# Attention values in two arrangements: partition halves exchanged by SP's DMA queue in place of VectorE copies

## The chip, the cores and the metric

The kernel runs on one core of a Trainium2 chip. A core has TensorE (PE: matrix multiplications from SBUF into PSUM), VectorE (DVE) and ScalarE (ACT) for elementwise work and for moving PSUM to SBUF, GpSimd (POOL) and SyncE (SP), here used to issue DMAs. Each engine runs its own instructions in order; semaphores order work between engines. DMAs issued by SP are carried out in the background by 16 DMA engines, which all queues share. SBUF and PSUM have 128 partitions; elementwise engines here read and write the same partition numbers or whole halves of 64. The metric is the device time of one execution, in microseconds (us).

## The reference

Inputs are q, k, v of shape (8 batches, 12 heads, 448 rows, 64) and three weights. For each batch and head

```python
scores = scale * np.matmul(q, k.transpose(0, 1, 3, 2))   # scale = 1/sqrt(64)
attn = np.maximum(scores, 0.0) ** 2 / S                  # S = 448
return np.matmul(attn, v)
```

The heads' outputs stand side by side as x of shape (8*448, 768), and the second part is

```python
gate = np.maximum(x @ w_gate, 0.0)      # 768 -> 1536
val = x @ w_val
return (gate * val @ w_out)             # 1536 -> 768, float32
```

## The kernel before

**Tiling.** Matmuls are done four at a time on the 64x64 quarters of the PE array (`mm4`, all through line 72). Two heads make a pair, two pairs a quad; a batch has three quads (qd 0 to 2). A score tile (`tile_of`, 21 in a batch, seven for each quad) is one `mm4` of 64x448 blocks into a pair of PSUM banks. `relu2` evacuates it: ACT takes the relu into an `r_sb` buffer (line 232), DVE squares it into `attn` (line 233). `r_sb` has four buffers (pool `rpool`), and a new relu needs a buffer whose last user has finished.

**Values.** When a quad's seven score tiles are done, seven `mm4` (28 matmuls, `value_passes`) accumulate its 128x2x448 values in a pair of PSUM banks. For batches 1 to 5, `values` evacuates them to `x0`, the first bank by ACT (line 266), the second by DVE (line 267); the gate and value matmuls also need `x1`, the same data with the two partition halves exchanged. `exchange` makes it with two DVE copies of 64x896 bf16 (line 261). Batch 0 is done by `first_batch`, which evacuates by itself and then calls `exchange`. For the last two batches, 6 and 7, `values_by_parity` makes two other arrangements: `even`, which holds the low half's values in both halves, and `odd`, which holds the high half's in both. Each engine evacuates its bank in two instructions, low half to `even` and high half to `odd` (lines 276 and 277), then DVE copies each across (lines 278 and 279).

**The order of the work.** The order on every engine is the program's (`pin`). Each body of the loop over batches (line 746) runs the gate and value units of the batch before (`gv_unit`: 12 steps of one `mm4`, then a relu on ACT at line 320 and a product on DVE at line 321) and, between their steps, the score tiles and values of the batch itself. `paced` places these events evenly. A value event of a quad stands two score tiles behind the quad's last one. Score tiles and value banks take turns in PSUM at banks 0-1 and 2-3 (`sc_later`), so each waits for the evacuation of the one two before it. In body 5 the attention of batch 6 begins early: (6,0), which is batch 6, quad 0, goes into a place in `kn_b[1]`; batch 7's x arrangements use `kr` and `qr`.

**Transposes.** From batch 2 on, q and k are regrouped on DVE (line 180, into `kr` and `qr`) and transposed into `T_b` by DMA transposes that SP issues: eight a batch, at places given by `turned` for batches 2, 4, 5, 6 and 7, and at the end of body 2 for batch 3. POOL issues most loads; a small POOL copy (`hold`, line 677) waits for a batch's transposes, and the next loads stand behind it. SP also stores half of the result in `out_pair` (line 409).

**The rest.** `out_pair` is the last product, done for two batches at once; batches 6 and 7 use a scheme with fewer products, prepared by `token_sums` and computed by `gv_pair`, which read the `even` and `odd` arrangements.

Of the kernel before, what the change touches and what calls it, by code (L numbers as in the profile page):

```python
# [10 lines left out]
BF16 = mybir.dt.bfloat16  # L11
AF = mybir.ActivationFunctionType
ALU = mybir.AluOpType
# [3 lines left out]
def kernel(  # L17
# [22 lines left out]
    nc = tc.nc  # L40

    B, H, S, D = q.shape
# [5 lines left out]
    NQ = HP // 2  # L48
# [4 lines left out]
    lam = 1.0 / (D * S)  # L53
# [5 lines left out]
    rpool = ctx.enter_context(tc.tile_pool(name="rpool", bufs=4))  # L59
# [6 lines left out]
    HALVES = [(c, slice(c * 64, c * 64 + 64)) for c in range(2)]  # L66

    def pin(ins):
        return tc.keep_in_program_order(ins)
# [181 lines left out]
    def value_passes(b, qd, ps, i0, i1):  # L251

        attn, v_sb = attn_of(b, qd), v_b[b % NB]
        for i in range(i0, i1):
            mm4([ps[:, r, :S] for r in range(2)], lambda r, c: v_sb[:, 2 * qd + c, i, :],
                lambda r, c: attn[:, 2 * i + c, :], i == 0, i == NC - 1)

    def exchange(b, qd):
        x0, x1 = (x_of[b][e][qd] for e in range(2))
        for (_, p), (_, other) in zip(HALVES, HALVES[::-1]):  # L260
            pin(nc.vector.tensor_copy(x1[p], x0[other]))  # L261

    def values(b, qd, ps):
        value_passes(b, qd, ps, 0, NC)
        x0 = x_of[b][0][qd]
        pin(nc.scalar.activation(x0[:, 0, :], ps[:, 0, :S], AF.Copy))  # L266
        pin(nc.vector.tensor_copy(x0[:, 1, :], ps[:, 1, :S]))
        exchange(b, qd)

    def values_by_parity(b, qd, ps):  # L270

        value_passes(b, qd, ps, 0, NC)
        even, odd = (x_of[b][e][qd] for e in range(2))
        lo, hi = (p for _, p in HALVES)
        for x, p in ((even, lo), (odd, hi)):
            pin(nc.scalar.activation(x[p, 0, :], ps[p, 0, :S], AF.Copy, scale=float(lam)))
            pin(nc.vector.tensor_scalar(x[p, 1, :], ps[p, 1, :S], float(lam), None, ALU.mult))
        pin(nc.vector.tensor_copy(even[hi], even[lo]))
        pin(nc.vector.tensor_copy(odd[lo], odd[hi]))
# [315 lines left out]
    def first_batch(units):  # L595
# [53 lines left out]
        passes(1, 4)  # L649
        value_passes(0, 2, both, 4, NC)  # L650
        exchange(0, 0)
        exchange(0, 1)
        pin(nc.scalar.activation(x_of[0][0][2], both[:, :, :S], AF.Copy))
        exchange(0, 2)
# [181 lines left out]
```

## Time and profile before

| what | value |
|---|---|
| median of 3 runs | 406.9 us (406.57 to 408.36) |
| profiled execution, its own time | 406.69 us |
| its span, first to last instruction | 404.9 us |
| PE busy | 393.0 us, 97% |
| DVE busy | 303.9 us, 75% |
| ACT busy | 244.3 us, 60% |
| SP's DMA queue (q1) | 13.99 MB, 17.9% of 16 engines |

The page gives, for each engine, the busy time and its share of the span; then groups of instructions by line, with what they wrote and read (`x<-x` is a tile x written from a tile x), how many there were, the time that they kept the engine busy, the mean length of one in ns, and the idle time before them with what ended it. A timeline lists instructions in order of start: start, length, engine, line, operation, output and inputs, shapes, and how many were merged; in square brackets stand the idle time before and the instruction or DMA that ended it. "SPq" is an instruction in SP's sequence, so its length is the time to issue a DMA; the landing is listed apart.

### The profile page before, as it was taken

Reading aid. Unit: us, or ns where it says so; the run is one execution under the profiler, and the core shown is the slowest. Engines: PE = TensorE matmul, PEld = TensorE weight load, DVE = VectorE, ACT = ScalarE, POOL = GpSimd, SP = SyncE. Lnnn points to the kernel's source line nnn. Section 1 sums busy time; section 2 is a strip of 40 time slices with the busy share of each in tenths; the row PEclk is TensorE's granted clock in tenths of the full one; section 3 lists DMA queues with packets and bytes.
Section 4 is the critical chain, followed back from the end, with each engine's and each line's share of the span. In section 5 each row is a group of like instructions: output and inputs, shape, how many; then the busy total and the mean of one; then the engine's idle time right before and its main releaser. Section 6 shows DMA issues by size and latency. Waiting matters only on the chain.

```text
span 404.9 us, 16604 instructions
## 1 busy us (share of the span) xinstructions
PE 393.0 (97%) x7392; PEld 276.3 (68%) x7392; DVE 303.9 (75%) x532; ACT 244.3 (60%) x358; POOL 96.0 (24%) x164
## 2 busy tenths in 40 slices
PE   7899999999999999999999999999999999999994
PEld 3567767779776666666677677687777766777773
DVE  5985895599944786787833988988889869997651
ACT  3962984797334776877324889899873243434221
POOL 8833500610213601205244030020003120000240
PEclk9999999999999999999999999999999999999999
DMA  9999999799726993978946459561002350000154
GB/s 157 176 196 196 197 194 135 122 203 162 119 83 177 118 161 70 139 112 99 191 86 173 103 88 123 103 95 14 3 3 50 83 145 3 3 2 3 42 135 101
DMA packets 90984, 44.17 MB, mean 109 GB/s; under 512 B 55424, under 2 KB 89952, under 8 KB 90912
## 3 DMA queue, kind: packets, MB, share of 16 engines
q0 software_dynamic: 51136, 28.58, 49.5%
q1 hardware_dynamic: 39104, 13.99, 17.9%
q8 instruction: 58, 0.95, 0.9%
q10 hardware_dynamic: 672, 0.54, 0.5%
q14 instruction: 14, 0.11, 0.1%
HBM read 47.19 MB, written 11.01 MB: 144 GB/s over the span
## 4 chain that ended last, share of the span: by engine, by line
PE 79%; DVE 7%; DMA 5%; ACT 3%; issue 2%; SPq 2%; POOL 0%; DVEq 0%; ACTq 0%; POOLq 0%
PE ps L72 78%; DVE attn L233 4%; DMA kn<-in_k_dram 3%; ACT r_sb L232 3%; SPq L409 2%; DMA qn<-in_q_dram 1%; PE ps L208 1%; DMA out_dram<-attn 1%; DVE x L640 1%; DVE attn L399 0%; DVE kqT L209 0%; DVE hT L321 0%; ACT g_sb L320 0%; DVE kr L180 0%; DVE qr L180 0%
## 5 line engine op out<-in xcount | busy, mean ns | idle before, releaser
L72 PE MATMUL ps<-x,gv 64*64 64x448 bf16 x3552 | 203.5, 349 | 0.5 <-ACT r_sb L232 0.3
L72 PEld LDWEIGHTS <-gv 64*64 64x64 bf16 x4032 | 139.0, 107 | 54.8 <-issue 2.8
L232 ACT ACTIVATE r_sb<-ps 128x896 bf16<-128x896 f32 x167 | 147.9, 926 | 18.6 <-PE ps L72 15.1
L233 DVE TENSOR_TENSOR attn<-r_sb 128x896 bf16<-128x896 bf16 x167 | 102.2, 623 | 31.3 <-ACT r_sb L232 24.5
L72 PE MATMUL ps<-kqT 64*64 64x448 bf16 x672 | 67.9, 351 | 3.8 <-ACT r_sb L232 2.8
L72 PEld LDWEIGHTS <-hT 128*64 128x64 bf16 x1056 | 56.2, 110 | 20.8 <-issue 1.7
L409 POOL DMA_DIRECT2D out_dram<-attn x60 | 31.6, 531 | 154.0 <-DVE attn L399 121.2
L395 ACT ACTIVATE attn<-ps 128x384 f32<-128x384 f32 x64 | 28.9, 451 | 63.9 <-PE ps L72 63.3
L72 PE MATMUL ps<-wo,hT 128*64 128x384 bf16 (+1 forms) x720 | 53.9, 306 | 0.0
L321 DVE TENSOR_TENSOR hT<-ps,g_sb 128x448 bf16<-128x448 f32 x72 | 44.5, 619 | 9.2 <-ACT g_sb L320 8.6
L320 ACT ACTIVATE g_sb<-ps 128x448 bf16<-128x448 f32 x72 | 39.2, 546 | 18.5 <-PE ps L72 18.1
L399 DVE TENSOR_TENSOR attn<-ps,attn 128x384 f32<-128x384 f32 (+1 forms) x48 | 22.7, 503 | 33.4 <-ACT attn L395 19.4
L72 PEld LDWEIGHTS <-vn 64*64 64x64 bf16 (+1 forms) x840 | 30.9, 107 | 12.8 <-issue 2.3
L72 PEld LDWEIGHTS <-kqT 64*64 64x64 bf16 x672 | 27.0, 106 | 18.4 <-issue 8.4
L72 PE MATMUL ps<-attn,vn 64*64 64x448 bf16 x672 | 36.9, 350 | 0.1
L513 ACT ACTIVATE kqT<-ps 128x896 f32<-128x896 f32 x18 | 16.5, 918 | 25.0 <-PE ps L72 25.0
L116 POOL DMA_DIRECT2D vn<-in_v_dram x36 | 23.8, 681 | 23.0 <-DMA wo<-in_moe_w_out_dram 9.6
L677 POOL COPY flag<-kqT 128x1 bf16<-128x1 bf16 x12 | 3.1, 261 | 103.0 <-DMA kqT<-kr 75.9
L72 PE MATMUL ps<-o_ring,hT 128*64 128x384 bf16 (+1 forms) x336 | 25.8, 306 | 0.1
L517 DVE TENSOR_TENSOR kqT<-ps,kqT 128x896 f32<-128x896 f32 x18 | 19.5, 1084 | 5.9 <-PE ps L72 4.2
L266 ACT ACTIVATE x<-ps 128x448 bf16<-128x448 f32 x15 | 8.2, 544 | 14.4 <-PE ps L72 14.4
L261 DVE COPY x<-x 64x896 bf16<-64x896 bf16 x36 | 14.7, 408 | 2.0
(104 smaller groups left out, 289.4 us busy)
## 6 DMA issues: line engine op xcount, KB each, us to landing
out_dram<-attn SPq DMA_DIRECT2D x48, 96.0 KB, 2.6
out_dram<-attn POOLq DMA_DIRECT2D x46, 96.0 KB, 2.4
kn<-in_k_dram POOLq DMA_DIRECT2D x7, 384.0 KB, 5.9
qn<-in_q_dram POOLq DMA_DIRECT2D x7, 384.0 KB, 7.8
vn<-in_v_dram POOLq DMA_DIRECT2D x14, 192.0 KB, 9.1
gv<-in_moe_w_gate_dram POOLq DMA_DIRECT2D x6, 384.0 KB, 11.3
gv<-in_moe_w_val_dram POOLq DMA_DIRECT2D x6, 384.0 KB, 10.9
wo<-in_moe_w_out_dram POOLq DMA_DIRECT2D x2, 1152.0 KB, 12.3
```

What stands on the lines that cost most here:

```text
L72: pin(nc.tensor.matmul(o, lhsT=l, rhs=r, start=start, stop=stop, skip_group_check=True))
L116: pin(nc.gpsimd.dma_start(out=o, in_=i))
L232: pin(nc.scalar.activation(r, src, AF.Relu))
L233: pin(nc.vector.tensor_tensor(dst, r, r, ALU.mult))
L261: pin(nc.vector.tensor_copy(x1[p], x0[other]))
L320: pin(nc.scalar.activation(g_sb, o[0], AF.Relu, scale=float(out_scale)))
L321: pin(nc.vector.tensor_tensor(hT[:, mf, col:col + S], o[1], g_sb, ALU.mult))
L395: pin(nc.scalar.activation(out_of(t, r, c), bank(P, t), AF.Copy))
L399: pin(nc.vector.tensor_tensor(o, bank(Q, t), o, ALU.add))
L409: pin(engines[c].dma_start(out=rows[:, c0:c1, :], in_=src))
L513: pin(nc.scalar.activation(held(n, j), both(PQ[n][0]), AF.Copy))
L517: pin(nc.vector.tensor_tensor(k, both(PQ[n][1]), k, ALU.add))
```

## The change

`exchange` issues its two copies as DMAs from SP for quads 0 and 1 of batches 1 to 5. Batch 0 and quad 2 of every batch keep DVE's copies.

`values_by_parity` evacuates both banks once over all 128 partitions, ACT the first and DVE the second, into a tile `both` that is allocated from `rpool` under the name `r_sb`; four DMAs from SP then copy each half of `both` to both halves of `even` or `odd`. Quad 2 of batch 7, the last, keeps the way of before.

```diff
     def exchange(b, qd):
         x0, x1 = (x_of[b][e][qd] for e in range(2))
         for (_, p), (_, other) in zip(HALVES, HALVES[::-1]):
-            pin(nc.vector.tensor_copy(x1[p], x0[other]))
+            if b > 0 and qd < NQ - 1:
+                pin(nc.sync.dma_start(out=x1[p], in_=x0[other]))
+            else:
+                pin(nc.vector.tensor_copy(x1[p], x0[other]))
...
         value_passes(b, qd, ps, 0, NC)
         even, odd = (x_of[b][e][qd] for e in range(2))
+        if (b, qd) != (B - 1, NQ - 1):
+            both = rpool.tile([128, 2, S], BF16, name="r_sb")
+            pin(nc.scalar.activation(both[:, 0, :], ps[:, 0, :S], AF.Copy, scale=float(lam)))
+            pin(nc.vector.tensor_scalar(both[:, 1, :], ps[:, 1, :S], float(lam), None, ALU.mult))
+            for x, (_, p) in zip((even, odd), HALVES):
+                for _, o in HALVES:
+                    pin(nc.sync.dma_start(out=x[o], in_=both[p]))
+            return
         lo, hi = (p for _, p in HALVES)
```

## The prediction

> **What bounds the kernel now.** I read the page first, then the chain of waits, then the timelines of SP, ACT and PE around the places that the change touches.
>
> ```profile
> span 404.9 us, 16604 instructions
> PE 393.0 (97%) x7392; PEld 276.3 (68%) x7392; DVE 303.9 (75%) x532; ACT 244.3 (60%) x358; POOL 96.0 (24%) x164
> ...
> L261 DVE COPY x<-x 64x896 bf16<-64x896 bf16 x36 | 14.7, 408 | 2.0
> ...
> out_dram<-attn SPq DMA_DIRECT2D x48, 96.0 KB, 2.6
> ```
>
> TensorE is busy for 97% of the span and DVE for 75%. So DVE time that is taken away is worth only what TensorE waits for DVE; every new wait of TensorE is paid in full. A DVE exchange copy takes 0.41 us, a plain copy issued by SP lands 2.6 us after its issue.
>
> The timeline of SP (start, length, what) has two places where the new copies get in behind transposes:
>
> ```profile
> 55.81 8.52 SPq L188 DMA_TRANSPOSE kqT<-kr  x4
> 64.38 7.10 SPq L188 DMA_TRANSPOSE kqT<-qr  x4
> ...
> 254.04 5.95 SPq L188 DMA_TRANSPOSE kqT<-kr  x4
> 260.08 6.03 SPq L188 DMA_TRANSPOSE kqT<-qr  x4
> ```
>
> SP issues in order, and eight transposes hold it for 12.1 us (254.04 to 266.11). The timelines of ACT and of PE in that stretch:
>
> ```profile
> 257.53 1.10 ACT L276 ACTIVATE kn<-ps 64x448 bf16<-64x448 f32 x2 [0.35 <-PE ps L72]
> 258.65 0.92 ACT L232 ACTIVATE r_sb<-ps 128x896 bf16<-128x896 f32 x1
> 260.23 0.92 ACT L232 ACTIVATE r_sb<-ps 128x896 bf16<-128x896 f32 x1 [0.66 <-PE ps L72]
> 261.05 0.54 ACT L320 ACTIVATE g_sb<-ps 128x448 bf16<-128x448 f32 x1
> 261.56 2.67 ACT L232 ACTIVATE r_sb<-ps 128x896 bf16<-128x896 f32 x3
> 264.12 0.55 ACT L320 ACTIVATE g_sb<-ps 128x448 bf16<-128x448 f32 x1
> 264.54 1.75 ACT L232 ACTIVATE r_sb<-ps 128x896 bf16<-128x896 f32 x2
> ```
>
> ```profile
> 259.82 0.38 PE L72 MATMUL ps<-kqT 64*64 64x448 bf16 x2 [0.63 <-DVE kn L277]
> ...
> 264.79 0.51 PE L72 MATMUL ps<-kqT 64*64 64x448 bf16 x4
> ...
> 265.53 1.52 PE L72 MATMUL ps<-attn,vn 64*64 64x448 bf16 x28
> ```
>
> The value bank of batch 6, quad 0 (written (6,0) below) is evacuated at 257.5, in the middle of the transposes of batch 7. Five relus of score tiles follow it: 258.65, 260.23, and three from 261.56; then, after a g_sb, those of tiles 14 and 15.
>
> **The change, part by part.** The compiled order of PE and of POOL is unchanged; DVE loses 24 rows, ACT four; SP gains 40 copies of 64x896 bf16 (112 KB each, 4.6 MB).
>
> *Work removed.* 20 exchange copies x 0.408 = 8.2 us of DVE. In five value banks two copies (0.39 each) and one of two TENSOR_SCALARs (0.62): 5 x 1.4 = 7.0 us of DVE; one of two 0.54 us activations: 2.7 us of ACT. DVE should fall from 303.9 to about 289, ACT to 241.6. On the path of this I find the 0.63 us above (TensorE waits for the second TENSOR_SCALAR; used below), 0.46 us at 287.77 (a score tile waits for a relu behind the two activations), some 0.3 us at 277 (the same kind) and some 0.4 us in gaps of 0.1 to 0.2 at 61, 238, 294 and 302. Together -1.2 us besides the 0.63; bounds 0 and -2.
>
> *(A) The bank copy of (6,0).* The new tile `both` is one of the four r_sb buffers, and its four DMAs must land before the buffer is used again. In the compiled order it is the fifth relu after it (tile 13) that waits for these four DMAs; in the trace that relu starts at 263.3. The DMAs stand in SP's order behind batch 7's transposes. Last transpose done with issuing: 266.12. SP's stores to HBM are the nearest row for a plain copy: 0.55 us each, 0.62 from start to start, so the fourth starts at 268.03. They landed after 1.9 to 4.2 us, median 2.2 in the stretch from 212 to 224; with 2.3 the buffer is free at 270.3, and tile 13's relu ends 0.92 later, at 271.25. Tile 15 writes the same PSUM banks as tile 13. It would have come at 264.79 - 0.65 = 264.14 (without the wait for the second TENSOR_SCALAR), and now waits until 271.25. Behind it on ACT are the g_sb and tile 14's relu, done at 272.6; the values of (6,1) need that one's banks. They began at 265.53 before: 7.1 us later.
>
> TensorE then stood still for about 7 us, and its clock counts. At the end of this trace the last matmul ends at 399.44, and the granted clock still reads 1.00 in 404.0 to 404.5 and 0.82 in 404.5 to 404.9, so it fell to half about 5.3 us after the last matmul. At the start, matmul pairs of the first row (from 1.16) go every 0.37 us until 5.27, and every 0.19 us from 7.3: 4.1 us at half speed. So I let the clock fall at about 269.6 and return at 275.4. In between lie 28 value matmuls (1.33 us, 2.65 at half speed) and little else that isn't waiting for ACT anyway: +1.4, bounds 0 and half of 4.1. Part A: +8.5 us, the 0.63 counted in. Its other bounds: eight transposes held SP for 11.3 us (from 226.65) to 15.7 us (from 55.81), so -0.8 to +3.6; a landing of 1.9 or 4.2, so -0.4 to +1.9. I take the row itself and the median, as the same transposes stand in the same place.
>
> *(B) The exchange of (1,1).* Batch 1's second exchange stands behind four transposes that issue until 64.33 and before the next four. Its first reader is the 41st matmul of a row that starts at 65.05, at 0.048 us each: 66.97. Issued at 64.4 and 65.0, the copies could land 2.3 us later, the second at 67.3: 0.3 us of stall. But the fourth transpose, issued at 63.07, landed 4.8 us later, at 67.87, and the next, issued at 64.38, 4.1 us later: landings on this queue keep their order there. Behind them the second copy lands about 68.4: +1.4, bounds +0.3 and +2.1 (4.1 after 65.0). The trace is nearer to the second, since DMA moves 143 to 194 GB/s there. The Trainium skill's page "DMA: Bandwidth & Descriptors", section "Anatomy of one DMA — SWDGE (gpsimd) path", has a fit of 2.0 us plus bytes over 436 GB/s: for 112 KB an estimate of 2.3 us, by which B is 0.3 and the sum 1.1 lower; the 4.1 and 4.8 us above differ from it, and I go by them. The same page, section "Queues, rings and completion order", says that a semaphore increment lands only after every earlier write of its DMA engine, which would hold these copies behind the transposes.
>
> *(C) Batch 1's first exchange* adds 224 KB at 50 us to loads that run at 194 GB/s. Natural k of batch 2 lands at 54.98 and DVE starts on it at 55.10, without a gap from there to the evacuation (57.65) that TensorE waits for at 58.3. The load is late by 0 to 224 KB / 194 GB/s = 1.2 us: I take +0.5.
>
> *(D) The other four banks.* (6,1) is evacuated by 267.74 (DVE 267.12 + 0.62); four DMAs on a free SP land at 267.8 + 3 x 0.62 + 2.3 = 272.0. Its fifth relu starts at about 272.3 in the trace of before. (7,0) and (7,1) have the same distance within 0.3, (6,2) a relu more. +0.2; bounds 0 and, with 4.2 us to land, some 5.
>
> *Hidden.* (3,1) waits for SP until 157.7, lands behind the last transpose (160.5) at about 161.1 and is first read at 162.33: covered by 1.2 us of scores. (2,0), (2,1), (3,0), (4,0), (4,1), (5,0), (5,1) land 20 us or more before use, or find SP free. The four transposes behind (1,1) come 1.2 us later, and POOL's check of them (72.66), behind which the next loads stand: k of batch 3 then lands at 93 for use at 97.4.
>
> Sum: +8.5 + 1.4 + 0.5 + 0.2 - 1.2 = +9.4 on the profiled execution's 406.69 us: 416.1, and its distance to the median of 406.9 is below what matters: 416.0.
>
> **Rivals.**
> 1. Faster: plain copies don't queue behind the transposes, as SP's rows might be issue work that overlaps. It decides at one point: the last copy of (6,0) lands before 262.7, when its relu is wanted (0.6 earlier than before). Then A is only the -0.63 and B is nothing: 406.7 - 0.63 - 1.2 = 404.9. For it: POOL's and SP's rings are several. Against it: the next issue starts only after the one before has ended in all rows of SP, and landings keep order.
> 2. The wait comes but costs less: clock not lost (-1.4), transposes through SP in 11.3 us (-0.8), B 0.3 (-1.1), more relief (-0.8): single or together 412 to 414.7.
> 3. The copies land as slowly as the slowest store, 4.2 us. (6,0) +1.9, (6,1) +1.9, (7,0) and (7,1) about +1 and +1.5, since their fifth relus start only 4.9 to 5.4 us after the evacuation: 422. For it: a source and a target in SBUF, which this trace hasn't got; against: 112 KB is little more than the stores' 96.
>
> **How the numbers follow.** Forecast 0.65 (own range 413 to 418.5), rival 1 0.05, rival 2 0.18, rival 3 0.12. The range of 411 to 420 leaves out rival 1 and most of rival 3 with a tail below 412. What counts as no change is within 0.5% (2.0 us), about what repeated runs can tell. Rival 1 is 1.8 us, so near that bound: faster 0.04; within 0.5% 0.03, with a mixture of rivals 1 and 2; slower 0.93.
>
> **What would show it.** A: a relu (L232) that waits for DMA for 6 to 8 us near 263, TensorE idle from about 264 to 271 (shifted by what came before), the clock down to 0.5 afterwards. B: a gap of 1 to 2 us of TensorE near 67, ended by DMA. The page: DVE near 289 us, q1 near 18.6 MB. The forecast is wrong if that relu finds its buffer free, if SP lets the copies pass, or if the copies land in 4 us or more.

## The result: 3.1% slower

| | before | changed |
|---|---|---|
| median of 6 runs each | 407.36 us | 420.27 us (418.53 to 421.92) |
| profiled execution, its own time | 406.69 us | 418.53 us |
| its span | 404.9 us | 416.8 us |
| DVE busy | 303.9 us | 289.0 us |
| ACT busy | 244.3 us | 242.3 us |
| mean granted clock | 1.00 | 0.987 |

The ratio is 1.031, with a 95% interval of 1.0279 to 1.0342. The median lies 0.3 us above the range of 411 to 420 that was forecast, on the side that was forecast; the ratio on the 406.9 us from which the forecast started gives 419.5, just inside it.

The page of the changed kernel, first lines and SP's queue:

```profile
span 416.8 us, 16622 instructions
PE 396.2 (95%) x7392; PEld 285.9 (69%) x7392; DVE 289.0 (69%) x497; ACT 242.3 (58%) x353; POOL 95.4 (23%) x164
...
PEclk9999999999999999999999999959999999999999
...
q1 hardware_dynamic: 42304, 18.58, 23.0%
```

DVE lost its 15 us, ACT its 2, the queue gained 4.6 MB: the change does what it says. Yet TensorE's share fell, and its clock row has a slice at half speed, the 27th of 40 (271 to 281 us). The timelines of SP, of ACT and of PE in that place:

```profile
255.54 6.10 SPq L188 DMA_TRANSPOSE kqT<-kr  x4
261.73 6.22 SPq L188 DMA_TRANSPOSE kqT<-qr  x4
268.12 2.39 SPq L283 DMA_DIRECT2D kn<-r_sb  x4
```

```profile
259.03 0.54 ACT L279 ACTIVATE r_sb<-ps 128x448 bf16<-128x448 f32 x1 [0.35 <-PE ps L72]
...
262.48 1.80 ACT L232 ACTIVATE r_sb<-ps 128x896 bf16<-128x896 f32 x2
273.73 0.92 ACT L232 ACTIVATE r_sb<-ps 128x896 bf16<-128x896 f32 x1 [9.46 <-DMA kn<-r_sb]
```

```profile
264.95 1.02 PE L72 MATMUL ps<-x,gv 64*64 64x448 bf16 x16
274.70 0.59 PE L72 MATMUL ps<-kqT 64*64 64x448 bf16 x4 [8.73 <-ACT r_sb L232]
...
275.95 2.83 PE L72 MATMUL ps<-attn,vn 64*64 64x448 bf16 x28
```

The bank of batch 6, quad 0 is evacuated from 259.0 to 260.6, ACT's half first. Its four copies start on SP only when the last transpose has been issued, at 268.12. The fifth relu after it waits 9.46 us for them, and TensorE, which needs that relu's PSUM banks, 8.73. The 28 value matmuls that follow take 2.83 us instead of 1.52: they run at half clock. The four copies' landings, and the load of v of batch 7 that POOL starts beside the last one:

```profile
DMA to landing us min/median/max: 2.1/2.2/3.7
```

```profile
269.81 2.64 POOL L116 DMA_DIRECT2D vn<-in_v_dram  x4 [0.33 <-issue]
```

Matmul by matmul (both kernels have the same 7392 in the same order), the lateness against the trace of before is built up in four places: 0.34 us by 58 us, 1.17 us at 67 us, 10.85 us between 258 and 280 us, and it falls by 0.58 us after that: 11.8 us in all.

### The profile page after: what moved, and what is told of

It is laid out like the page before. It is cut to its first block, busy times and chain, and to the rows that moved or that the text cites. A ratio compares the mean times of both kernels' runs of the same rounds, so it can differ in the third digit from the quotient of the medians.

```text
span 416.8 us, 16622 instructions
## 1 busy us (share of the span) xinstructions
PE 396.2 (95%) x7392; PEld 285.9 (69%) x7392; DVE 289.0 (69%) x497; ACT 242.3 (58%) x353; POOL 95.4 (23%) x164
## 4 chain that ended last, share of the span: by engine, by line
PE 75%; DMA 13%; POOL 3%; ACT 2%; SPq 2%; DVE 2%; issue 1%; ACTq 0%; POOLq 0%; DVEq 0%
PE ps L72 75%; DMA gv<-in_moe_w_val_dram 6%; DMA kn<-in_k_dram 3%; ACT r_sb L232 2%; SPq L188 1%; POOL vn L116 1%; DMA x<-x 1%; DMA kn<-r_sb 1%; POOL qn L116 1%; DMA x<-r_sb 1%; SPq L283 1%; DMA qr<-r_sb 1%; POOL gv L116 1%; DVE attn L233 1%; POOL kn L116 0%
## 5 line engine op out<-in xcount | busy, mean ns | idle before, releaser
L72 PE MATMUL ps<-x,gv 64*64 64x448 bf16 x3552 | 206.2, 351 | 1.1 <-DMA x<-x 0.7
L72 PEld LDWEIGHTS <-gv 64*64 64x64 bf16 x4032 | 149.3, 107 | 50.4 <-issue 4.0
L72 PE MATMUL ps<-kqT 64*64 64x448 bf16 x672 | 72.6, 354 | 11.9 <-ACT r_sb L232 11.1
L72 PEld LDWEIGHTS <-kqT 64*64 64x64 bf16 x672 | 30.6, 107 | 25.2 <-issue 16.3
L72 PEld LDWEIGHTS <-vn 64*64 64x64 bf16 (+1 forms) x840 | 33.2, 109 | 12.8 <-issue 2.7
L72 PE MATMUL ps<-attn,vn 64*64 64x448 bf16 x672 | 39.3, 359 | 0.3
L116 POOL DMA_DIRECT2D qn<-in_q_dram x20 | 14.6, 750 | 1.1 <-POOLq L831 0.8
```

The costliest lines, as they stand in the source:

```text
L72: pin(nc.tensor.matmul(o, lhsT=l, rhs=r, start=start, stop=stop, skip_group_check=True))
L116: pin(nc.gpsimd.dma_start(out=o, in_=i))
```

## Experiments

Two theories went into the first four. Theory 1: one relu buffer is held by copies that come late because SP is busy with transposes. Theory 2: all forty copies cost something.

**The exchanges alone.** The value banks are evacuated as before.

```diff
-        if (b, qd) != (B - 1, NQ - 1):
+        if False:
```

> The exchange of batches 1 to 5 by SP's DMAs as in the change; the value banks of batches 6 and 7 evacuated as before. Theory 1 (the held buffer): nearly all of the loss is one relu's wait for the bank copies of batch 6, quad 0, which stand behind eight transposes on SP; the exchanges cost only what the trace of the change shows near 58 us (0.34) and near 67 us (1.17): 1.5 us over the kernel before, TensorE idle for about 1 us near 67, none of more than 1 us near 264, clock 1.00 throughout. Theory 2 (every copy costs, by shared DMA engines and SP's issue): 20 of the 40 copies are here, so about half of the 12 us, +6 us, spread over batches 1 to 5.

Measured: 409.37 us beside 408.15 of the kernel before, ratio 1.0028 (1.0007 to 1.0049); the span is 2.5 us longer in the profiled execution. TensorE's timeline, and a line of DVE's:

```profile
59.02 0.38 PE L72 MATMUL ps<-kqT 64*64 64x448 bf16 x2 [1.04 <-DVE x L270]
...
69.18 1.13 PE L72 MATMUL ps<-x,gv 64*64 64x448 bf16 x14 [1.33 <-DMA x<-x]
```

```profile
55.80 0.56 DVE L180 COPY kr<-kn 128x1536 bf16<-128x1536 bf16 x1 [0.94 <-DMA kn<-in_k_dram]
```

Both stalls are batch 1's. The first is the evacuation that stands behind the natural k that came late (DVE waited 0.94 us for it), the second the exchange behind the transposes. After 70 us this trace and the one of before keep the same distance to within 0.3 us. So the other sixteen copies cost nothing that shows, and theory 2 falls for the exchanges.

**The banks alone.** The exchange is DVE's again.

```diff
-            if b > 0 and qd < NQ - 1:
+            if False:
```

> The value banks of batches 6 and 7 as in the change, the exchange by DVE as before. Theory 1: +10.3 us over the kernel before (the 11.8 us by which the last matmul of the change is late, less the 1.5 of the exchanges), a single gap of TensorE of 8 to 10 us near 264, the clock at half for about 10 us from then on. Theory 2: the other 20 copies, +6 us, with stalls at all five banks.

Measured: 417.20 us, ratio 1.0219 (1.0176 to 1.0263), some 9 us; the matmuls end 9.5 us late. Both are a little under the 10.3 us expected, and the clock was at half for 6.8 us, not 10. The timeline of ACT:

```profile
271.86 0.92 ACT L232 ACTIVATE r_sb<-ps 128x896 bf16<-128x896 f32 x1 [9.43 <-DMA kn<-r_sb]
```

It is one wait of the same size, with one gap of TensorE of 8.7 us; the only other relu that waits for a bank's copies does so for 1.5 us, at 308 us. In the profiled executions the two halves (2.6 and 9.5 us at the last matmul) add up to about the change's 11.8. By the medians they fall short of it: the two ratios multiplied give 1.025, where the change has 1.031. This, however, doesn't yet say which property of that wait matters: the buffer, or the place in SP's queue.

**Another buffer for the first bank.** Batch 6, quad 0 goes into an unused part of natural k.

```diff
-            both = rpool.tile([128, 2, S], BF16, name="r_sb")
+            both = (flat(kn_b[1], 6, S)[:, 4:6, :] if (b, qd) == (B - 2, 0)
+                    else rpool.tile([128, 2, S], BF16, name="r_sb"))
```

> As the change, but for batch 6, quad 0 the tile for the whole bank lies in an unused part of the natural k buffer instead of one of the four relu buffers; its DMAs stay behind the transposes on SP. Theory 1: the copies land as late as before (near 272), and nobody waits: no relu waits for DMA for more than 1 us near 264, TensorE's gap there is under 1 us, the clock stays at 1.00; +0.5 to +1 us over the kernel before (1.5 of the exchanges less 0.65 and some 0.4 of relief of DVE and ACT at the banks). If it were the late data itself, or the copies' load on the DMA engines, that matters: the loss stays at 10 us or more.

Measured: 415.17 us, ratio 1.0184 (1.0127 to 1.024). The wait at 264 is gone, as theory 1 has it, but the time isn't: about 7 us of loss stay. The timelines of ACT, POOL and PE show a second place, where a relu is wanted at 273.0, some 9 us after the first:

```profile
278.71 1.73 ACT L232 ACTIVATE r_sb<-ps 128x896 bf16<-128x896 f32 x2 [5.70 <-DMA x<-r_sb]
```

```profile
269.30 0.19 POOL L688 COPY flag<-kqT 128x1 bf16<-128x1 bf16 x1 [6.15 <-DMA kqT<-qr]
269.81 2.64 POOL L116 DMA_DIRECT2D vn<-in_v_dram  x4 [0.33 <-PE ps L72]
```

```profile
279.67 0.59 PE L72 MATMUL ps<-kqT 64*64 64x448 bf16 x4 [5.21 <-ACT r_sb L232]
```

Now it is quad 1's buffer. Its four copies, issued from 270.6 to 273.1, landed after 4.6 to 6.4 us. At 269.3 POOL saw that the transposes had landed and let the load of v of batch 7 go. In the changed kernel TensorE stood still during that load, so quad 1's copies came after it (issued from 279.5, landed after 2.2 to 3.5 us): the first stall had covered the second. Theory 1 was too narrow.

**Another queue for the first bank.** The relu buffer is kept, and POOL issues the four copies.

```diff
-                    pin(nc.sync.dma_start(out=x[o], in_=both[p]))
+                    pin((nc.gpsimd if (b, qd) == (B - 2, 0) else nc.sync).dma_start(out=x[o], in_=both[p]))
```

> As the change, but the four copies of batch 6, quad 0 are issued by POOL, whose queue is free there, from the same relu buffer. Theory 1 (the place behind the transposes on SP is what makes the copies late): evacuated near 259.6, four issues of 0.7 us, landed 2.4 us after the last one starts: near 264.5, when the fifth relu is wanted at 264.2; a wait of ACT of under 1 us, +0.5 to +1.5 us over the kernel before. Rival: four relu buffers are too few for any copies by DMA, on whatever queue: the relu waits for 3 us or more, +4 us or more.

Measured: 416.63 us, ratio 1.0198 (1.015 to 1.0247). Theory 1's number is missed, and the rival's wait is there. POOL's timeline and the landings of its copies, then ACT's timeline:

```profile
261.29 0.55 POOL L283 DMA_DIRECT2D kn<-r_sb  x1 [14.19 <-ACT r_sb L232]
262.07 1.57 POOL L283 DMA_DIRECT2D kn<-r_sb  x3 [0.23 <-issue]
```

```profile
DMA to landing us min/median/max: 3.1/4.3/5.9
```

```profile
269.15 0.92 ACT L232 ACTIVATE r_sb<-ps 128x896 bf16<-128x896 f32 x1 [4.80 <-DMA kn<-r_sb]
...
281.24 1.73 ACT L232 ACTIVATE r_sb<-ps 128x896 bf16<-128x896 f32 x2 [1.89 <-DMA x<-r_sb]
```

The copies are issued 7 us earlier and land only 4.6 us earlier: beside eight transposes they take 3.1 to 5.9 us, where copies on a quiet machine take 2.2. So SP's order is about half of the first delay. Of the 4.8 us that are left, about 3.7 is the slower landing of the last copy (an estimate: 5.9 us instead of 2.2) and 1 the issuing of four. That it is the transposes' traffic on the shared DMA engines which slows the landing is argued, not shown by a run of its own; POOL's queue by itself isn't slow, as its stores of 96 KB land after 2.5 us (median) in this run. The expectation also took the bank as evacuated 1 us too early: DVE's half was done at 260.7.

Theory 1 now read (1a in the expectations): a relu buffer is held by copies that land late, for quad 0 behind and beside the transposes, for quad 1 beside the load that the transposes release.

**The load of v later.** As the run with another buffer for the first bank, with one more wait ahead of that load.

```diff
-            events += [(3, 1, lambda: (hold(7), load_v(7)))]
+            events += [(3, 1, lambda: (hold(7), hold_unit(5, 2), load_v(7)))]
```

> As the run with only batch 6, quad 0 in another buffer (there quad 1's copies landed 4.6 to 6.4 us after their issue, and a relu waited 5.7 us for them), with the load of v of batch 7 held back until unit 2 of that body is done, about 3 us later. Theory 1a (that load is what makes quad 1's copies slow): they land 2.2 to 3 us after their issue, which stays late (270.6 to 273.1) behind quad 0's copies; the relu that wants its buffer at 273 waits 2 to 3.5 us, not 5.7, and TensorE 2 to 3; +3 to +4.5 us over the kernel before, against about 7. Rival (SP's queue alone makes them late): the wait stays at 5 us or more.

Measured: 411.36 us, ratio 1.011 (1.0065 to 1.0156), against 1.0184 without the delay. The profiled execution is the fastest of the four (408.48 us at a mean clock of 0.997; the slowest has 414.61 at 0.990), so the median holds more than the trace shows. POOL's timeline, SP's copies with their landings, and ACT's timeline:

```profile
273.46 2.64 POOL L116 DMA_DIRECT2D vn<-in_v_dram  x4 [0.30 <-issue]
```

```profile
L283 SPq DMA_DIRECT2D x<-r_sb x4: 533/596/1262, 270.2 to 272.8; - x4
...
DMA to landing us min/median/max: 2.3/3.0/3.3
```

```profile
275.22 1.73 ACT L232 ACTIVATE r_sb<-ps 128x896 bf16<-128x896 f32 x2 [2.20 <-DMA x<-r_sb]
```

With the load started at 273.5 instead of 269.8, quad 1's copies land in 2.3 to 3.3 us instead of 4.6 to 6.4, and the wait falls from 5.7 to 2.2. The load is what slowed them. Most of what remains is their place behind quad 0's four copies: the bank was evacuated by 268.7 and SP was free at 270.2, 1.5 of the 2.2 us. TensorE's gap there was 1.7 us, a little under the 2 to 3 expected.

**All banks in other buffers.** Natural q and k are free from the last regroup to the token sums, and hold all five.

```diff
-            both = rpool.tile([128, 2, S], BF16, name="r_sb")
+            both = flat((kn_b, qn_b)[b - (B - 2)][0], HP, S)[:, 2 * qd:2 * qd + 2, :]
```

> As the change, but all five whole-bank tiles of batches 6 and 7 lie in the natural q and k buffers (unused from the last regroup to the token sums), so that no relu ever waits for a copy. Theory 1a (one cause, two places: a relu buffer is held by copies that land late, behind SP's transposes for quad 0 and beside the loads of v of batch 7 for quad 1): copies land as late as in the other runs and nobody waits; no gap of TensorE of over 1 us after 70 us, clock 1.00; what is left is the exchange of batch 1 (1.5 to 2.5 us) less 1.1 of relief: +0.5 to +1.5 us over the kernel before. Rival (the copies' load on the DMA engines delays something else, v of batch 7 or the transposes, that TensorE needs): +4 us or more stay.

Measured: 407.02 us beside 408.25, ratio 0.9981 (0.9958 to 1.0003). The expectation of +0.5 to +1.5 us is missed on the fast side; in the profiled execution the matmuls end 0.15 us late. The copies of the first two quads still land late, and no relu waits for them:

```profile
DMA to landing us min/median/max: 2.1/4.5/7.3
```

TensorE's longest waits in this run and in the changed kernel:

```profile
PE ps L72 <- ACT r_sb L232: 2.7, 7, 0.6
PE ps L72 <- DMA x<-x: 1.2, 1, 1.2
```

```profile
PE ps L72 <- ACT r_sb L232: 11.4, 8, 8.7
```

With the same copies in the same queues and only the five banks' tiles in other buffers, the loss is gone. The rival, that the copies' load delays other work, falls.

**The same, without batch 1's exchange by DMA.**

```diff
-            if b > 0 and qd < NQ - 1:
+            if b > 1 and qd < NQ - 1:
```

> As the run with all banks in other buffers, and batch 1's exchange by DVE again (batches 2 to 5 by SP's DMAs). Theory 1a: the stalls at 58 and 67 us are those of before; only the relief is left: -0.5 to -1.2 us against the kernel before, no gap of TensorE over 1 us after 20 us. Rival: batches 2 to 5's exchanges cost too: 0 to +1 us.

Measured: ratio 0.9963 (0.9936 to 0.999). The matmuls end 1.3 us early, where 0.5 to 1.2 was expected; batches 2 to 5's exchanges cost nothing that shows.

**The same, every exchange by DVE.**

```diff
-            if b > 0 and qd < NQ - 1:
+            if False:
```

> The banks of batches 6 and 7 evacuated whole into other buffers and spread by SP's DMAs, every exchange by DVE as before: the part of the change that relieves TensorE, without its waits. Theory 1a: -0.5 to -1.2 us against the kernel before, the stalls of 0.8 us near 260 and 0.6 us near 288 gone or down to 0.2. Rival: relief of ACT and DVE is worth nothing since other waits end at the same time: within 0.3 us.

Measured: 406.07 us beside 408.25, ratio 0.9952 (0.9931 to 0.9973); the medians differ by 2.2 us, where 0.5 to 1.2 was expected, and the matmuls end 1.1 us early in the profiled execution. That trace loses 1.0 us near 65 us, where TensorE waits for nothing that the profile shows, and gains 2.0 from 250 us on. PE's timeline has, without an idle time in brackets, the two tiles that waited 0.63 and 0.46 us before:

```profile
259.71 0.73 PE L72 MATMUL ps<-kqT 64*64 64x448 bf16 x4
...
286.87 0.38 PE L72 MATMUL ps<-kqT 64*64 64x448 bf16 x4
```

This version and the one before beat the kernel before by 0.4 to 0.5%; their intervals don't tell them apart. What they keep is the whole-bank evacuation.

## Why the prediction was right, and where its sizes were off

- **Work removed.** DVE 289.0 us as forecast, ACT 242.3 against 241.6. The rows that went are 35 of DVE and five of ACT, as the forecast's own sum has them, not the 24 and four that it names. The relief of TensorE is there where it was read, in times of the trace of before: 0.65 us at 260, 0.35 at 277 and 0.6 at 288. The estimate of 1.2 besides the first is matched by the three runs with all banks in other buffers (1.4, 1.1 and 1.4 us between 250 us and the end); in the changed kernel itself only 0.6 net is left after 280 us, as quad 1's copies (up to 3.5 us to land) held a relu for 0.56 us.
- **(A), the bank of (6,0).** Right in every link: the transposes, the held buffer, the fifth relu, tile 15, the clock. The size was 8.5 and measured 10.85; the relu waited 9.46 us, where 6 to 8 was named as the sign. Of the difference, 1.4 us is the fourth copy, which landed 3.7 us after its issue instead of 2.3, beside the load of v that POOL had released at 269.8 (with that load at 273.5, no copy of this bank took more than 2.4); the term "landing" was sized from a stretch in which SP's and POOL's stores ran, and no load or transpose. Some 0.4 us is SP, done with transposes that much later than the stalls before account for. The rest, about 0.5 us, is the clock.
- **The clock.** Forecast: down 5.3 us after the last matmul, back 4.1 us after work resumes, cost 1.4. The last matmul before the gap ended at 265.97, the clock fell near 269.7 (0.84 in 269 to 270) and rose near 279.9 (0.58 in 279.5 to 280): 3.7 us to fall, 5.2 us of work at half speed, of which the 4.0 from the value matmuls on cost 1.9.
- **(B), the exchange of (1,1).** Forecast 1.4, measured 1.17 in the changed kernel, 1.8 with the exchanges alone, and 0.7 to 1.8 over the six runs that have it. The copies landed 3.5 and 3.8 us after their issue, behind the transposes; the 2.3 us by the fit that the prediction quotes from the Trainium skill (page "DMA: Bandwidth & Descriptors") was too short here.
- **(C), batch 1's first exchange.** Forecast 0.5, measured 0.4 in the changed kernel and 1.0 with the exchanges alone, where DVE waited 0.38 and 0.94 us for the natural k: the path is as forecast.
- **(D), the other banks.** Forecast +0.2. Right in sum for the changed kernel by luck, and wrong as a statement on the banks: SP was free for (6,1) only since (A) had moved it by 10 us. With (A) taken away, (6,1) cost TensorE a wait of 5.2 us, and 7.7 with the half clock behind it. The forecast took each bank's cost on the timeline of before, with SP free at 267.8; with (6,0)'s copies queued until 270.5 it never was.
- **The forecast time.** 9.4 us against 11.8 in the profiled execution. The rest of the distance to the median is the spread of the changed kernel's runs (418.5 to 421.9), of which the profiled one was the fastest; what makes the others slower is open. The result lies between the forecast and rival 3's 422, in part for rival 3's reason, a copy that lands late, though only one of these four did.

## What to carry to other kernels

A copy moved from an engine to a DMA keeps its source buffer for as long as the queue ahead of it and the traffic beside it last: ask whose buffer that is, before asking who needs the result. With the banks in buffers of their own, forty copies cost here no more than the relieved engines gave back; with the banks in the ring of four that the next relus needed, they cost 12 us. When a stall is taken away, look again at what it had kept apart: here it had held the next copies back until a load was over.

## What was not expected of the hardware

The half clock came in whole windows. Mean clock by stretch (length, busy times, clock in the third column from the end), in the run with POOL's copies, where TensorE stood from 266.0 to 270.1:

```profile
270.00:271.00 1.00, 0.76 (x12) 0.39 (x12) 0.90 (x2) 1.00 (x3) 0.19 (x1) 1.00 0.00 0
271.00:272.00 1.00, 0.64 (x8) 0.42 (x11) 0.89 (x2) 1.00 (x2) 0.75 (x2) 0.51 0.00 0
272.00:274.00 2.00, 2.00 (x28) 1.24 (x24) 0.62 (x1) 0.12 (x1) 1.58 (x3) 0.50 0.64 75
274.00:275.00 1.00, 1.00 (x24) 0.71 (x20) 0.62 (x1) 0.78 (x2) 0.35 (x1) 0.78 1.47 180
```

A gap of 4.1 us was enough, and the clock fell near 271.0, when TensorE was working again, to come back near 274.4: 3.4 us. In the 3.4 us before the fall TensorE stood for 2.5 and worked again for the last 0.9. After gaps of 5.2, 8.7 and 8.7 us it was down for 6.8 us (the run with one other buffer, the banks alone) and 10.2 us (the changed kernel): two and three times 3.4. With a gap of 1.7 us (the load of v later) it stayed at 1.00 from 270 to 290. The Trainium skill's page "TensorE: Matmul & The Clock Gate", section "Part 1: The HAM clock gate", says that activity is judged in free-running windows of 3.4 us; these lengths agree, and such windows would explain why the 5.3 and 4.1 us read from the two ends of the trace of before were no fixed delays.

A copy of 112 KB from SBUF to SBUF took 2.2 us from issue to landing on a quiet machine, like the stores, 3.1 to 5.9 beside transposes, 4.6 to 6.4 beside a load of v, and 5.4 to 6.7 beside the loads at 50 us.
